# Attention in steps of two groups, with the second mix and the scores on four 64x64 quarters of TensorE

## The chip, the cores and the metric

The kernel runs on one core of one Trainium2 chip. The metric is the device time of one execution in microseconds (us), and the median over several runs is compared. The engines are named as the profile names them: PE (TensorE matmul) and PEld (its weight loads), DVE (VectorE), ACT (ScalarE), POOL (GpSimd) and SP (SyncE, which here only issues DMAs).

## What is computed

An attention with two mixes over the heads, then two feed-forward layers, all in float32 at the interface. There are 4 batches, 12 heads, 448 rows, head dimension 64. The output of the attention is laid out as 1792 rows by 768 columns.

```python
scores = scale * np.matmul(q, k.transpose(0, 1, 3, 2))
scores = np.einsum('bhij,hg->bgij', scores, w_pre)
scores = scores - np.max(scores, axis=-1, keepdims=True)
attn = np.exp(scores)
attn = attn / (np.sum(attn, axis=-1, keepdims=True) + 1e-09)
attn = np.einsum('bhij,hg->bgij', attn, w_post)
x = np.matmul(attn, v)              # then to (1792, 768)
x = (sigmoid(x @ w_gate) * (x @ w_val)) @ w_out
out = np.maximum(x @ w_in2, 0) ** 2 @ w_out2
```

## The kernel before

**Order of the work.** Two programs share the engines. The attention (function attention) is written out by hand as a loop over groups of ten query rows. The two feed-forward layers (function mlp) are built as a list of tasks, and the class Feed emits each task into an engine's queue when its own model of the engines says there is room. During the attention the call feed.step(2.4) after each group (line 448) lets the feed emit 2.4 us worth of its model's time. What it emits there is the preparation of the first layer's weights: loads of raw weights (line 786), two ACT passes (lines 790 and 793), a DVE shift (796), POOL additions (802), DVE or POOL combinations (824) and stores to DRAM (831). The first twelve of these conversions, two halves each, feed the first layer. The layers' own matmuls all stand at line 926 and are not emitted before Feed.finish (line 672) or, on the feed's PE clock, not before that clock is set there.

**Attention, one group at a time.** The 448 rows of a batch are cut into 4 tiles of 100 or 120 rows, ten rows to a group: 45 groups a batch, 180 in all.

- scores (line 188): for one pair of heads and one tile, two float32 matmuls, 64 rows of the array by the tile's 100 or 120 columns, moving 448 columns (line 201). ACT copies one head's result out of PSUM (213), DVE the other's (211), and each goes by one DMA on the SP queue into the buffer g (223), which holds all 12 heads of five query rows on 64 partitions.
- premix (229): the first mix over heads. For two groups at once, four matmuls of 64x64, one in each quarter of the array (237).
- maximum (245), exponent (251), normal (258): row maximum on DVE (248), exp with a sum on ACT (255), sum plus 1e-9 and reciprocal on DVE (260, 263), and the second mixing matrix scaled by the reciprocals on POOL (266).
- postmix (275): the second mix, which also transposes. A group has 128 partitions, two halves of five rows by 12 heads each; the scaled matrix wn is 128 x 120 and is zero where the half of the partitions is not that of the row. Four matmuls with weights of 128 x 112 and 120 moving columns (282). mixed (291) copies the result from PSUM into ap (294).
- values (304): for a chunk of two tiles and a pair of heads, eight matmuls with weights of 112 x 64, moving 240 or 208 columns (311). valued (322) copies on ACT (326) and stores to xs (327).

A float32 matmul shows as two matmul records and two weight loads in the trace. PSUM has eight banks: two for scores (ps_q), four for premix (ps_m), two shared by postmix and values (ps_b).

**What sets the order.** Group s runs premix, maximum(s), exponent(s-1), normal(s-2). Scores and the back part (postmix at least LAG = 3 groups later, and values) are put in by a running budget, left_over, with a cost for each kind of work (lines 29 and 402 to 442). Scores of the next tile are all made LA = 3 groups before the tile begins.

Of the kernel before, what the change touches and what calls it, by code (L numbers as in the profile page):

```python
# [9 lines left out]
F32 = mybir.dt.float32  # L10
# [9 lines left out]
P = 128  # L20
JP = 112
GI = 10
HV = 2
LAG = 3
LA = 3
NA = 9
HB = GI // 2
HP = P // 2
MW, PW, VW, SW, STEP = 0.40, 0.85, 1.66, 0.92, 2.2
# [4 lines left out]
def row_tiles(S):  # L34

    n = -(-S // (2 * GI))
    cuts = [0]
    for t in range(4):
        cuts.append(min(cuts[-1] + (n // 4 + ((0, 1, 3, 2)[t] < n % 4)) * 2 * GI, S))
    return list(zip(cuts, cuts[1:]))  # L40


def columns(i0, i1):

    return 2 * -(-(i1 - i0) // (2 * GI))


def blocks(b, i0, i1):

    n = columns(i0, i1)  # L50
    return [(0, 4), (4, n)] if b == i0 == 0 else [(0, n)]


def row_order(b, i0, i1):

    rows = []
    for g0, g1 in blocks(b, i0, i1):  # L60
        for y in range(2):
            for r in range(HB):
                for g in range(g0, g1):
                    rows.append(min(i0 + (g // 2 * 2 + y) * GI + g % 2 * HB + r, i1 - 1))
    return rows


def attention(tc, feed, q, k, v, w_pre, w_post, xs, B, H, S, D):
# [11 lines left out]
    JT = S // JP  # L80
    NP = H // 2
    SCALE = 1.0 / float(D) ** 0.5

    tiles, groups, chunks = [], [], []
    for b in range(B):
        for t, (i0, i1) in enumerate(row_tiles(S)):
            if t % 2 == 0:
                chunks.append([b, i0, i1, len(groups), 0])
            for g0 in range(i0, i1, GI):
                groups.append((len(tiles), g0 - i0, min(GI, i1 - g0), len(chunks) - 1, g0))  # L90
            chunks[-1][2] = i1
            chunks[-1][4] = len(groups)
            tiles.append((b, i0, i1 - i0))
    NG = len(groups)
    full = [columns(0, t[2]) * GI for t in tiles]
    IM = max(full)
    GT = IM // GI
    CM = max(c[2] - c[1] for c in chunks)
# [3 lines left out]
    with ExitStack() as ctx, ExitStack() as mid, ExitStack() as left:  # L102
        kw = dict(side="right")
        one = ctx.enter_context(tc.tile_pool(name="a_one", bufs=1, **kw))
        pv4 = ctx.enter_context(tc.tile_pool(name="a_v", bufs=4, **kw))
        po = ctx.enter_context(tc.tile_pool(name="a_o", bufs=4, **kw))
        pp = ctx.enter_context(tc.tile_pool(name="a_p", bufs=1, **kw))
        pa = mid.enter_context(tc.tile_pool(name="a_a", bufs=NA, **kw))
        pg = mid.enter_context(tc.tile_pool(name="a_g", bufs=1, **kw))
        ps_b = ctx.enter_context(tc.tile_pool(name="ps_b", bufs=2, space=PSUM, **kw))  # L110
        ps_q = mid.enter_context(tc.tile_pool(name="ps_q", bufs=2, space=PSUM, side="left"))
        ps_m = mid.enter_context(tc.tile_pool(name="ps_m", bufs=4, space=PSUM, side="left"))
        pk = left.enter_context(tc.tile_pool(name="a_k", bufs=KB, side="left"))
        p2 = left.enter_context(tc.tile_pool(name="a_2", bufs=2, side="left"))
        p4 = left.enter_context(tc.tile_pool(name="a_4", bufs=3, side="left"))
# [4 lines left out]
        wq = one.tile([P, H, GI], F32, name="wq")  # L120

        wr = p0.tile([P, 2, H], F32, name="wr")
        mask = p0.tile([P, GI, H], F32, name="mask")
        first = p0.tile([HP, HB, H], F32, name="first")
        g_of = [pg.tile([P, GT, S], F32, name=f"g{m}") for m in range(2)]

        def masks():
# [5 lines left out]
            nc.sync.dma_start(  # L133
                out=wr[G0 : G0 + GI * H, 0, :], in_=w_pre.unsqueeze(0).to_broadcast([GI, H, H])
            )
            for u in range(2):
                nc.sync.dma_start(
                    out=wr[u * HP : u * HP + KH, 1, :],
                    in_=w_post.unsqueeze(0).to_broadcast([HB, H, H]),
                )  # L140
            for u, m in ((0, first), (0, mask[:HP, :HB]), (1, mask[HP:, HB:])):
# [13 lines left out]
        def mixers():  # L155
            for u, m in enumerate((first, mask[HP:, HB:])):
# [9 lines left out]
                in1=wr[:, 1:2, :].to_broadcast([P, GI, H]),  # L166
# [4 lines left out]
        k_t, q_t = {}, {}  # L171
# [5 lines left out]
        def q_load(n, p0=0, p1=NP):  # L177
            if p0 == 0:
                q_t[n] = p2.tile([P, NP, IM], F32, tag="q", name="q")
            n0, isz = sum(full[:n]) * H * D, full[n]  # L180
# [3 lines left out]


        g_t, second = {}, []

        def scores(n, p):

            b, i0, rows = tiles[n]  # L190
            isz = full[n]
            if p == 0:
                g_t[n] = g_of[n % 2]
            kt = k_t.pop((b, p)) if i0 + rows == S else k_t[b, p]
            ps = [
                ps_q.tile([P, S], F32, tag="q", name="ps_s")
                for _ in range(2)
            ]
            for o in range(2):
                r = slice(o * D, (o + 1) * D)  # L200
                nc.tensor.matmul(  # L201
                    ps[o][:isz], lhsT=q_t[n][r, p, :isz], rhs=kt[r], start=True, stop=True
                )
            if n == 0 and p >= 3:
                e = [pa.tile([IM, S], F32, tag="a", name="e0") for _ in range(2)]
            else:
                t = p4.tile([IM, 2, S], F32, tag="e", name="e")
                e = [t[:, o] for o in range(2)]
            for o in range(2):
                if o:  # L210
                    nc.vector.tensor_copy(e[o][:isz], ps[o][:isz])  # L211
                else:
                    nc.scalar.copy(e[o][:isz], ps[o][:isz])  # L213
                e0 = 0
                to = g_t[n][G0 : G0 + GI * H].rearrange("(r h) g j -> h r g j", h=H)
                for m, (g0, g1) in enumerate(blocks(b, i0, i0 + rows)):
                    e1 = e0 + (g1 - g0) * GI
                    move = (to[2 * p + o, :, g0:g1], e[o][e0:e1])
                    if m:
                        second.append(move)  # L220
                    else:
                        queue = nc.scalar if n == 0 and o and p in (1, 3, 4, 5) else nc.sync
                        queue.dma_start(out=move[0], in_=move[1])
                    e0 = e1
# [4 lines left out]
        def premix(s):  # L229
            n, r0 = groups[s][:2]  # L230
            t = r0 // (2 * GI)
            for y in range(2):
                if s + y < NG and groups[s + y][0] == n:
                    a_t[s + y] = ps = ps_m.tile([P, S], F32, tag="m", name="ps_m")
                    r = slice(y * HP, HP + y * KH)
                    for u in range(2):
                        nc.tensor.matmul(  # L237
                            ps[u * HP : (u + 1) * HP],
                            lhsT=wp[r],
                            rhs=g_t[n][r, 2 * t + u],  # L240
                            start=True,
                            stop=True,
                        )

        def maximum(s):
            ps = a_t[s]
            nm = pa.tile([P, 1], F32, tag="nm", name="nm")
            nc.vector.tensor_reduce(out=nm, in_=ps, op=ALU.max, axis=AX.X, negate=True)  # L248
            a_t[s] = [ps, nm]

        def exponent(s):
            ps, nm = a_t[s]
            a = pa.tile([P, S], F32, tag="a", name="a")
            sm = pa.tile([P, 1], F32, tag="sm", name="sm")
            nc.scalar.activation(a, ps, AF.Exp, bias=nm, accum_out=sm)  # L255
            a_t[s] = [a, sm]

        def normal(s):
            sm = a_t[s][1]
            nc.vector.tensor_scalar(  # L260
                out=sm, in0=sm, scalar1=1e-9, scalar2=None, op0=ALU.add
            )
            nc.vector.reciprocal(out=sm, in_=sm)  # L263
            wn = pa.tile([P, H, GI], F32, tag="wn", name="wn")
            if s < NG - 14:
                nc.gpsimd.tensor_scalar(  # L266
                    out=wn, in0=wq, scalar1=sm, scalar2=None, op0=ALU.mult
                )
            else:
                nc.scalar.mul(wn, wq, sm)  # L270
            a_t[s] = [a_t[s][0], wn]

        ap, pending = {}, []

        def postmix(s):
            rows, c = groups[s][2:4]
            if s == chunks[c][3]:
                ap[c] = pp.tile([JP, JT, H, CM], F32, tag="ap", name="ap")
            a, wn = a_t.pop(s)
            ps = ps_b.tile([P, JT, H, GI], F32, tag="b", name="ps_p")  # L280
            for jt in range(JT):
                nc.tensor.matmul(  # L282
                    ps[:JP, jt],
                    lhsT=a[:, jt * JP : (jt + 1) * JP],
# [19 lines left out]
        def values(c, h):  # L304
# [13 lines left out]
            if (h + 2) % HV == 0:  # L318
                del vraw[c, h // HV]
# [945 lines left out]
```

## Time and profile before

| | |
|---|---|
| time before, median of 3 runs | 1388.54 us (1384.6 to 1390.13) |
| the profiled execution | 1390.98 us |
| its span, first to last instruction | 1389.2 us |
| first matmul of the layers in a full stream | about 488 us after the start |
| from there to the end | 901 us |

The span is the part of the execution between the first and the last instruction; 1.8 us of the profiled execution lie outside. In the profile a group of instructions has one row with its count, its busy time and the mean duration of one. Durations of neighbouring matmuls overlap, since the engine is pipelined: where a price is wanted, the distance between starts or the length of a run of matmuls is used, not the mean.

### The profile page before, as it was taken

What the parts mean: (1) busy time and instruction counts of PE and PEld (TensorE: products, weight loads), DVE (VectorE), ACT (ScalarE), POOL (GpSimd) and SP (SyncE); (2) the same over time, 40 slices, a digit from 0 to 9 for tenths busy, and PEclk for the clock granted to TensorE, in tenths of its full rate; (3) what the DMA queues carried; (4) which work ended last, traced back from release to release, by engine and by line L of the source; (5) the groups of instructions that cost most, each with busy time, mean ns of one, the idle gap of its engine ahead of it and who ended that gap; (6) DMA issues with size and microseconds to landing.
All of it is one profiled execution on the core that took longest, in us unless ns stands there. A gap on an engine that the chain in (4) does not pass through costs nothing.

```text
span 1389.2 us, 22066 instructions
## 1 busy us (share of the span) xinstructions
PE 1330.3 (96%) x7602; PEld 1067.5 (77%) x7602; DVE 962.3 (69%) x1828; ACT 709.9 (51%) x1373; POOL 330.1 (24%) x373
## 2 busy tenths in 40 slices
PE   6889999998999899999999999999999999999998
PEld 2445555564655679888999999999888999999998
DVE  2768686695877965677655688848688556898612
ACT  2544455454555655657556563845556445436620
POOL 3233353353444303242323200122231000000000
PEclk9999999999999999999999999999999999999999
DMA  4768878768777567777777742265885344342122
GB/s 153 228 217 249 238 211 269 229 205 256 215 246 222 198 189 271 261 247 260 264 239 253 278 128 57 85 214 171 302 258 195 115 120 142 99 155 58 57 85 80
DMA packets 134362, 268.06 MB, mean 193 GB/s; under 512 B 16684, under 2 KB 79084, under 8 KB 134252
## 3 DMA queue, kind: packets, MB, share of 16 engines
q1 hardware_dynamic: 133872, 266.09, 60.0%
q8 instruction: 60, 0.98, 0.3%
q10 hardware_dynamic: 380, 0.57, 0.1%
q14 instruction: 50, 0.41, 0.1%
HBM read 162.36 MB, written 64.68 MB: 163 GB/s over the span
## 4 chain that ended last, share of the span: by engine, by line
PE 82%; DMA 7%; DVE 7%; ACT 1%; issue 1%; POOL 1%; SPq 0%; DVEq 0%; ACTq 0%; POOLq 0%
PE ps L926 60%; PE ps_p L282 9%; PE ps_s L201 5%; PE ps_m L237 4%; PE ps_v L311 4%; DMA vraw<-in_v 3%; DMA g<-e 3%; DVE ap L294 1%; DVE c L942 1%; DVE w L900 1%; DVE nm L248 1%; DMA gv<-y 1%; DVE c L913 1%; DVE e L211 1%; POOL wn L266 0%
## 5 line engine op out<-in xcount | busy, mean ns | idle before, releaser
L926 PE MATMUL ps<-c,w 128*128 128x448 f32 x4290 | 883.7, 367 | 13.9 <-DVE w L900 6.1
L926 PEld LDWEIGHTS ps<-c,w 128*128 128x128 f32 x4290 | 805.3, 188 | 92.3 <-DVE w L900 10.5
L900 DVE TENSOR_TENSOR w<-w,w 128x768 fp32r<-128x768 f32 x189 | 194.7, 1033 | 173.2 <-ACT w L897 171.8
L802 POOL TENSOR_TENSOR y<-y,raw 128x384 int32<-128x384 int32 x136 | 151.5, 1133 | 433.4 <-DVE y L796 235.6
L897 ACT CAST w<-w 128x768 fp32r<-128x768 f32 x189 | 157.0, 834 | 151.5 <-PE ps L926 138.3
L282 PEld LDWEIGHTS ps_p<-wn,a 128*112 128x112 f32 x1440 | 158.2, 178 | 92.0 <-issue 37.3
L282 PE MATMUL ps_p<-wn,a 128*112 128x120 f32 x1440 | 183.4, 276 | 14.9 <-POOL wn L266 6.7
L913 DVE TENSOR_TENSOR c<-c 128x448 fp32r<-128x448 f32 x280 | 169.1, 647 | 16.2 <-ACT c L910 14.1
L910 ACT CAST c<-c 128x448 fp32r<-128x448 f32 x280 | 143.9, 564 | 55.0 <-DVE c L942 50.8
L266 POOL TENSOR_SCALAR wn<-wq,sm 128x120 f32<-128x120 f32 x166 | 106.5, 642 | 271.0 <-DVE sm L263 207.2
L942 DVE TENSOR_TENSOR c<-ps,c 128x448 f32<-128x448 f32 x172 | 106.6, 622 | 84.4 <-PE ps L926 66.2
L248 DVE TENSOR_REDUCE nm<-ps_m 128x1 f32<-128x448 f32 x180 | 111.0, 617 | 62.0 <-PE ps_m L237 61.7
L255 ACT ACTIVATE a<-ps_m,nm 128x448 f32<-128x448 f32 x180 | 114.5, 636 | 54.2 <-DVE sm L260 43.7
L294 DVE COPY ap<-ps_p 112x480 f32<-112x480 f32 x180 | 114.4, 649 | 18.9 <-PE ps_p L282 17.3
L201 PE MATMUL ps_s<-k,q 64*120 64x448 f32 (+1 forms) x384 | 105.9, 623 | 10.8 <-ACT e L213 5.3
L942 DVE TENSOR_TENSOR c<-c 128x448 f32<-128x448 f32 x184 | 113.0, 647 | 2.4 <-PE ps L926 0.6
L213 ACT COPY e<-ps_s 120x448 f32<-120x448 f32 (+1 forms) x96 | 51.1, 533 | 123.0 <-PE ps_s L201 88.0
L950 ACT COPY c<-ps 128x448 f32<-128x448 f32 x128 | 67.7, 534 | 76.7 <-PE ps L926 74.0
L237 PE MATMUL ps_m<-g,wp 64*64 64x448 f32 x720 | 94.2, 584 | 5.1 <-DMA g<-e 3.8
L311 PE MATMUL ps_v<-ap,vraw 112*64 112x240 f32 (+1 forms) x768 | 84.2, 365 | 10.5 <-DMA vraw<-in_v 9.7
L311 PEld LDWEIGHTS ps_v<-ap,vraw 112*64 112x64 f32 x768 | 54.5, 139 | 51.2 <-issue 15.0
L211 DVE COPY e<-ps_s 120x448 f32<-120x448 f32 (+1 forms) x96 | 60.0, 625 | 47.3 <-PE ps_s L201 29.6
(34 smaller groups left out, 535.3 us busy)
## 6 DMA issues: line engine op xcount, KB each, us to landing
w<-gv SPq DMA_DIRECT2D x84, 384.0 KB
g<-e SPq DMA_DIRECT2D x132, 210.0 KB
raw<-in_wo SPq DMA_DIRECT2D x56, 384.0 KB
w<-wi SPq DMA_DIRECT2D x56, 384.0 KB
w<-wo SPq DMA_DIRECT2D x49, 384.0 KB
wo<-y SPq DMA_DIRECT2D x42, 384.0 KB
gv<-y SPq DMA_DIRECT2D x36, 384.0 KB
raw<-in_wi SPq DMA_DIRECT2D x32, 384.0 KB
```

The costliest lines, as they stand in the source:

```text
L201: nc.tensor.matmul(ps[o][:isz], lhsT=q_t[n][r, p, :isz], rhs=kt[r], start=True, stop=True)
L237: nc.tensor.matmul(ps[u * HP : (u + 1) * HP], lhsT=wp[r], rhs=g_t[n][r, 2 * t + u], start=True, stop=True,)
L282: nc.tensor.matmul(ps[:JP, jt], lhsT=a[:, jt * JP : (jt + 1) * JP], rhs=wn.rearrange("p g i -> p (g i)"), start=True, stop=True,)
L294: nc.vector.tensor_copy(ap[c][:, :, :, g0 - i0 : g0 - i0 + rows], ps[:JP, :, :, :rows])
L311: nc.tensor.matmul(ps[o * D : (o + 1) * D, :w], lhsT=vraw[c, (h + o) // HV][:, (h + o) % HV, jt, :], rhs=ap[c][:, jt, h + o, :w], start=jt ...
L802: e.tensor_tensor(out=y3, in0=y3, in1=of(raw.tile.bitcast(I32)[:, :, 0])[:, i], op=ALU.add)
L897: e.copy(dst.tile[:, 0], flat())
L900: e.tensor_tensor(out=dst.tile[:, 1], in0=flat(), in1=dst.tile[:, 0].bitcast(F32), op=ALU.subtract)
L910: e.copy(hi.tile, src.tile)
L913: e.tensor_tensor(out=lo.tile, in0=src.tile, in1=hi.tile.bitcast(F32), op=ALU.subtract)
L926: e.matmul(bank.tile, lhsT=a[k], rhs=x[l], start=start and n == 0, stop=stop and n == 2, skip_group_check=more,)
L942: e.tensor_tensor(out=out.tile, in0=a.tile, in1=b.tile, op=op)
```

## The change

The attention is rewritten; the layers stay as they are.

- **Tiles and steps.** The work goes in steps of two groups (20 rows), 23 a batch and 92 in all. Batch 0 has five tiles of 3, 5, 5, 5 and 5 steps, the others four of 6, 6, 6 and 5: 17 tiles.
- **Scores** run as four matmuls of 64 rows by at most 64 columns, one in each quarter. After the first tile and part of the second, one ACT copy takes both heads out of PSUM (896 elements a partition); DVE no longer copies any. The DMAs into g stay as they were, two to a pair of heads.
- **Maximum, sum and reciprocal** are one DVE instruction for both groups of a step; exp stays at two a step.
- **Second mix.** The scaled matrix is 128 x 60 without its zero blocks. A step has 28 matmuls with weights of 64 x 64 and 60 moving columns: 7 blocks of 64 keys, 2 halves, 2 groups. One DVE copy of 960 elements a partition replaces two of 480. The result has 128 keys to a partition block instead of 112, with the keys of the last block filled up.
- **Values** take one tile and six heads at a time: 24 matmuls, weights 128 x 64, moving 120 columns (100 for a tile of five steps), and one ACT copy of three pairs. There are two such units a tile, 34 in all. The loads of v are two a batch instead of twelve.
- **PSUM.** Premix has two pairs of banks. Postmix, values and scores take turns on two other pairs (next_turn), in the order in which they are written.
- **Order.** The budget is gone. A fixed plan gives a step its scores (by the length of the tile before: 2, 2, 1, 1, 0, 0 or 2, 2, 1, 1, 0 or 1, 1, 0) and its values (in the fourth and fifth step of the next tile). Within a step TensorE gets premix, postmix of three steps before, values, scores.
- **Feed.** It gets 3.8 us of its model's time a step, from the fourth step on, and 1.5 us in each of twelve steps behind the last. The layers' matmuls may be emitted from the last step on. Four of the layers' PSUM banks come free at that point, where six did; the number of cells handed over early is 20 where it was 23.

```diff
+STEP = 2 * GI
+LAG = 3
+NA = 4
+EB = 4
...
+    lengths = [n // 4 + (t < n % 4) for t in range(4)]
+    if b == 0:
+        lengths = [3] + [(n - 3) // 4 + (t < (n - 3) % 4) for t in range(4)]
...
+        ps_t = ctx.enter_context(tc.tile_pool(name="ps_t", bufs=1, space=PSUM, **kw))
+        ps_m = mix.enter_context(tc.tile_pool(name="ps_m", bufs=2, space=PSUM, side="left"))
...
+        turns = [ps_t.tile([P, 2, BANK], F32, name=f"turn{m}") for m in range(2)]
...
+        def scores(n, p, ps, early=False):
...
+            for c in range(0, isz, HP):
+                c1 = min(c + HP, isz)
+                for o in range(2):
+                    r = slice(o * D, (o + 1) * D)
+                    nc.tensor.matmul(
+                        ps[c:c1, o, :S], lhsT=q_t[n][r, p, c:c1], rhs=kt[r], start=True, stop=True
+                    )
...
+                nc.scalar.copy(e[:isz], ps[:isz, :, :S])
...
+        def postmix(s):
+            n, t, ys = steps[s]
+            a, wn = a_t.pop(s)
+            ps = next_turn()
+            out = ps[:, :, : JT * 2 * KH].rearrange("p u (j y x) -> p u j y x", j=JT, y=2)
+            for y in ys:
+                for j in range(JB):
+                    c = j % 2 * HP
                     for u in range(2):
+                        r = slice(u * HP, (u + 1) * HP)
                         nc.tensor.matmul(
+                            out[c : c + HP, u, j // 2, y],
+                            lhsT=a[r, y, j * HP : (j + 1) * HP],
+                            rhs=wn[r, y].rearrange("p g i -> p (g i)"),
                             start=True,
                             stop=True,
                         )
...
+            for m in range(VP):
+                for j in range(JT):
+                    for o in range(2):
+                        nc.tensor.matmul(
+                            ps[o * D : (o + 1) * D, 0, m * 2 * c : (m + 1) * 2 * c],
+                            lhsT=vt[:, 2 * m + o, j],
+                            rhs=x[:, j, :, (i * VP + m) * 2 + o],
...
+            spread = {3: (1, 1, 0), 5: (2, 2, 1, 1, 0), 6: (2, 2, 1, 1, 0, 0)}[s1 - s0]
...
+            if 3 <= s < NS:
+                feed.step(3.8)
+            elif s >= NS:
+                feed.step(1.5)
...
-        self.free["PE"] = self.now
+        self.free["PE"] = max(self.free["PE"], self.now)
```

## Rows read from the trace of the kernel before

**Rows 1.** The page: the span, and each engine's busy time and share.

```profile
span 1389.2 us, 22066 instructions
PE 1330.3 (96%) x7602; PEld 1067.5 (77%) x7602; DVE 962.3 (69%) x1828; ACT 709.9 (51%) x1373; POOL 330.1 (24%) x373
```

**Rows 2.** Windows: length; PE, PEld, DVE, ACT, POOL busy; clock; DMA share; GB/s.

```profile
45.00:440.00 395.00, 372.31 (x2806) 219.94 (x2804) 294.88 (x767) 198.26 (x485) 158.17 (x216) 0.98 0.75 231
...
488.00:1389.00 901.00, 883.62 (x4290) 805.20 (x4290) 611.23 (x932) 470.79 (x789) 138.11 (x116) 1.00 0.54 176
```

**Rows 3.** The chain that ended last, by line, from the page.

```profile
PE ps L926 60%; PE ps_p L282 9%; PE ps_s L201 5%; PE ps_m L237 4%; PE ps_v L311 4%; DMA vraw<-in_v 3%; DMA g<-e 3%; DVE ap L294 1%; DVE c L942 1%; DVE w L900 1%; DVE nm L248 1%; DMA gv<-y 1%; DVE c L913 1%; DVE e L211 1%; POOL wn L266 0%
```

**Rows 4.** Groups by form, 45 to 440 us: busy, mean ns, idle before and releaser.

```profile
L282 PE MATMUL ps_p<-wn,a 128*112 128x120 f32 x1232 | 157.2, 276 | 8.7 <-POOL wn L266 4.9 <-DVE ap L294 3.3
L282 PEld LDWEIGHTS ps_p<-wn,a 128*112 128x112 f32 x1232 | 135.5, 178 | 76.1 <-issue 35.0 <-POOL wn L266 29.6 <-POOL y L802 8.1
...
L255 ACT ACTIVATE a<-ps_m,nm 128x448 f32<-128x448 f32 x156 | 99.3, 637 | 52.8 <-DVE sm L260 43.0 <-PE ps_p L282 6.3 <-DVE sm L263 1.5
L248 DVE TENSOR_REDUCE nm<-ps_m 128x1 f32<-128x448 f32 x157 | 96.9, 617 | 52.9 <-PE ps_m L237 52.7
L294 DVE COPY ap<-ps_p 112x480 f32<-112x480 f32 x151 | 96.2, 651 | 15.7 <-PE ps_p L282 14.3
...
L211 DVE COPY e<-ps_s 120x448 f32<-120x448 f32 x60 | 37.5, 625 | 21.7 <-PE ps_s L201 11.8 <-DMA g<-e 6.8 <-DMA k<-in_k 1.1
L213 ACT COPY e<-ps_s 120x448 f32<-120x448 f32 x60 | 32.0, 533 | 65.9 <-PE ps_s L201 45.4 <-DMA g<-e 12.0 <-issue 6.8
L255 ACT ACTIVATION_READ_ACCUMULATOR a<-ps_m,nm 128x1 f32 x156 | 31.1, 200 | 0.0
...
L263 DVE RECIPROCAL sm<-sm 128x1 f32<-128x1 f32 x157 | 25.7, 164 | 5.4
...
L790 ACT ACTIVATE raw<-raw 128x768 f32<-128x768 f32 x24 | 22.0, 917 | 0.0
...
L237 PEld LDWEIGHTS ps_m<-g,wp 64*64 64x64 f32 x316 | 15.7, 134 | 16.7 <-issue 8.8 <-ACT a L255 1.4
...
L326 ACT COPY xo<-ps_v 128x240 f32<-128x240 f32 x20 | 7.2, 360 | 26.2 <-PE ps_v L311 19.9 <-issue 5.6 <-ACT a L255 0.7
```

**Rows 5.** Pieces of the chain in order of time: start, length (us), what.

```profile
19.44 2.68 DMA g<-e
...
55.14 7.79 DMA g<-e
...
319.42 1.77 PE ps_v L311 x16
...
342.42 1.82 PE ps_p L282 x16
...
347.16 1.00 PE ps_p L282 x8
```

**Rows 6.** Timeline of PE, 338 to 352 us: start, length, records of one kind.

```profile
345.24 0.98 PE L237 MATMUL ps_m<-g,wp 64*64 64x448 f32 x8
346.15 1.02 PE L201 MATMUL ps_s<-k,q 64*120 64x448 f32 x4
347.09 1.07 PE L282 MATMUL ps_p<-wn,a 128*112 128x120 f32 x8
```

**Rows 7.** Timeline cut to what starts from 345.230 to 345.262 us.

```profile
345.23 0.15 PEld L237 LDWEIGHTS ps_m<-g,wp 64*64 64x64 f32 x4
345.24 0.61 PE L237 MATMUL ps_m<-g,wp 64*64 64x448 f32 x4
```

**Rows 8.** Timeline of the first premix, 22.5 to 24.4 us.

```profile
22.58 1.77 PE L237 MATMUL ps_m<-g,wp 64*64 64x448 f32 x8 [3.83 <-DMA g<-e]
```

**Rows 9.** Instructions of the scores' copies: duration ns min/median/max, first and last start.

```profile
L223 SPq DMA_DIRECT2D g<-e x188: 748/762/1698, 7.8 to 442.6; - x188
```

More of the change, by code (lines that the diff above doesn't have):

```diff
@@ L79, in attention @@
     nc = tc.nc
-    JT = S // JP
     NP = H // 2
+    JB = S // HP
+    JT = -(-JB // 2)
     SCALE = 1.0 / float(D) ** 0.5
-    tiles, groups, chunks = [], [], []
+    VP = 3
+    tiles, steps, starts = [], [], []
     for b in range(B):
[L86 to L93, printed above, removed]
@@ L94, in attention @@
-    NG = len(groups)
-    full = [columns(0, t[2]) * GI for t in tiles]
-    IM = max(full)
+        for i0, i1, length in row_tiles(b, S):
+            lead = skipped(i0, i1, length)
+            starts.append(len(steps))
+            for t in range(length):
+                steps.append((len(tiles), t, [y for y in range(2) if y * length * GI + (t + 1) * GI > lead]))
+            tiles.append((b, i0, i1, length, lead))
+    NT, NS = len(tiles), len(steps)
+    starts.append(NS)
+    sizes = [t[3] * STEP for t in tiles]
@@ L183, in q_load @@
             nc.sync.dma_start(out=q_t[n][:, p0:p1, :isz], in_=x[:, p0:p1])
[L186 to L198, printed above, removed]
-            for o in range(2):
[L200 to L224, printed above, removed]
@@ L273, in attention @@
[L273 to L284, printed above, removed]
-                    rhs=wn.rearrange("p g i -> p (g i)"),
-                    start=True,
-                    stop=True,
-                )
-            pending.append((mixed, s, ps))
@@ L322, in valued @@
-        def valued(c, h, ps):
-            b, i0, i1 = chunks[c][:3]
-            w = i1 - i0
-            xo = po.tile([P, CM], F32, tag="xo", name="xo")
-            nc.scalar.copy(xo[:, :w], ps[:, :w])
-            nc.sync.dma_start(out=xs[b][h * D : (h + 2) * D, i0:i1], in_=xo[:, :w])
-            if i1 == S and h + 2 == H:
-                feed.fire(("x", b))
-        NT = len(tiles)
-        starts = [next(s for s in range(NG) if groups[s][0] == n) for n in range(NT)] + [NG]
-        k_order = iter([(b, p) for b in range(B) for p in range(NP)])
@@ L384, in attention @@
-        for s in range(NG + 30):
-            if s < NG and groups[s][1] // GI % 2 == 0:
+            scores(0, p, [*spare, *turns][p % 4], True)
+            if p == 0:
+                mixers()
+        for p in range(NP - sum(x[0] == "scores" for s in range(starts[1]) for x in plan[s])):
+            scores(1, p, next_turn())
+        q_load(2)
+        k_next = {}
+        for n in range(NT):
+            if not last_of(n) or n + 1 == NT:
+                continue
+            b = tiles[n][0] + 1
+            first_free = KB - NP
+            for p in range(NP):
+                at = starts[n - 1] + 1 + p // 2 if p < first_free else starts[n - 1] + 2 + p // 2
+                k_next.setdefault(at, []).append((b, p))
@@ L439, in attention @@
[L439 to L449 removed]
+            if 1 <= s <= NS:
+                exponent(s - 1)
+                if s == NS:
+                    mix.close()
+                    low.close()
+                    feed.widen(1)
+                    feed.free["PE"] = feed.now
@@ new lines, in attention @@
+            after = []
+            if LAG <= s < NS + LAG:
+                after.append(postmix(s - LAG))
+            for x in k_next.get(s, ()):
+                k_load(*x)
+            for x in v_next.get(s, ()):
+                v_load(*x)
+            units = plan[s]
+            for f, *x in units:
+                if f == "values":
+                    after.append(values(*x))
+                    while len(after) > 1:
+                        after.pop(0)()
+            for f, *x in units:
+                if f == "scores":
+                    if after:
+                        after.pop(0)()
+                    n, p = x
+                    scores(n, p, next_turn())
+                    if p == NP - 1 and n + 2 < NT:
+                        q_load(n + 2)
+                    if n == NT - 1 and p == NP - 1:
+                        left.close()
+                        closed = True
+                        feed.widen(0)
```

360 lines of the change are left out of this document (162 added, 198 removed).

## The prediction

> **What bounds the kernel now.** The page comes first: of a span of 1389.2 us PE is busy 96%, and no other engine over 69% [rows 1]. That is a mean over two stages, so the windows come next [rows 2]. From 488 us on only the two layers run: 901 us with PE busy 883.6. The change leaves them as they are, so what it can win lies ahead of 488 us. In the attention's body, 45 to 440 us, PE is busy 372 of 395 us, DVE 295, ACT 198, POOL 158, the DMA engines 75%, at a granted clock of 0.98. The chain that ended last says the same [rows 3]: after the layers' matmuls, the second mix is the longest line (9%), then the scores, the first mix and the values; DMA takes some 7%. In the groups by form [rows 4] nearly every group on ACT and DVE waits for PE, and PE's second mix waits only 8.7 us in all. So the attention is bound by TensorE, with DVE some way behind.
>
> **The price of a column.** The 16 records of two second mixes in a row take 1.82 us and the 8 records of one take 1.00 [rows 5], so 8 more records of 120 columns cost 0.82 us: 0.103 us each, 0.85 ns a column. Sixteen records of the values, two column halves side by side, give the same: 8 x 240 x 0.85 ns is 1.64 us of their 1.77. A score or a first mix, two records of 448 columns in each part of the array, is then 0.77 us. From start to start they take 0.91 and 0.94 us [rows 6], so each change of shape costs some 0.15 us. The price of a weight load follows from 178 ns for 112 columns and 134 ns for 64 [rows 4]: 0.92 ns a column, 0.059 us for 64.
>
> **The second mix, which carries the sum.** Removed: 16 records a step, 1.82 us. Added: 28 matmuls, so 56 records, of 60 columns (0.051 us) with loads of 64 (0.059 us), over four quarters. The fullest quarter has 16 records. If the quarters work side by side and each hides a load behind the matmul before it, it takes 16 x 0.059 = 0.94 us; by columns alone it would be 0.82. If they do not work side by side, it is 56 x 0.059 = 3.3 us. The nearest row is the first mix, of the same 64 x 64 shape: its eight records, four quarters by two, take 0.98 us [rows 6], while one after another they would need 8 x 448 x 0.85 ns = 3.1 us. So I take 0.94, and keep 0.82 and 3.3 as ends.
>
> **A rule against it.** Can so many short matmuls be issued? The first mix's four matmuls all start between 345.230 and 345.262 us, with their four loads [rows 7]: at most 11 ns apart. At that distance the 56 records need 0.6 us and issue is no bound. The Trainium skill, TensorE: Matmul & The Clock Gate, section "Wait — 56ns, not 53.3ns?", says that start-to-start "never drops below ≈25 ns however small N is"; by that the step's second mix would be at least 1.4 us. The trace speaks against it for different quarters, but shows no run of more than four starts. I go by the row.
>
> **The other work on PE, for a step.** First mix 0.77; a score 0.77, and with the second mix now of the same shape the 0.15 us between them goes. A unit of values is 24 matmuls in two column halves, 24 records a half of 120 columns: 2.46 us, and 0.3 for the two changes of shape, 2.76. The columns are as before; only records and loads double, and 0.059 hides behind 0.103.
>
> **ACT.** Two exps with their sum reads, 2 x (0.637 + 0.200) = 1.67 us a step [rows 4]. A score's one copy of 896 elements lies between 0.53 (as the copy of 448) and 1.07 (two of them); 0.533 for 448 and 0.360 for 240 elements give 0.83 ns an element, so 0.91. The values' copy of 360 elements is 0.46 by the same slope. The weight conversions' 24 halves, two passes of 0.917 us, are 44 us, or 0.48 a step.
>
> **DVE and POOL.** DVE loses the scores' copies (0.625 us each, off PE's path already). What stays is at most 2 x 0.617 for the maximum, 2 x 0.651 for the copy out of the second mix and about 0.3 for the sums, 2.85 us a step; joined instructions save some of that and the conversions add some: I take 3.0. POOL was idle more than half of the time [rows 2] and its matrices shrink by half; nothing is charged.
>
> **The steps of a tile.** PE and ACT are not loaded in the same steps, and PE can be only some two steps ahead of ACT (two pairs of banks for the first mix), so a step costs about what its busiest engine does:
> - first and second step, two scores each: PE 0.77 + 0.94 + 1.54 = 3.25, ACT 1.67 + 1.82 + 0.48 = 3.97. ACT, 3.97.
> - third, one score: PE 2.48, ACT 3.06.
> - fourth, a score and values: PE 0.77 + 0.94 + 0.77 + 2.76 = 5.24.
> - fifth, values: PE 4.47.
> - sixth, neither: PE 1.71, DVE 3.0.
>
> A tile of six steps is 23.7 us, of five 20.7, the first one of three some 9.3. Nine, seven and one of them give 213 + 145 + 9 = 367 us.
>
> **What is late next.** A tile's first mix needs all 12 heads in g. After a tile of five steps the last score is written at the end of its fourth step; then come the copy (0.91), two issues on SP at 0.762 us each [rows 9] and a transfer that takes 2.7 to 7.8 us in the chain [rows 5]: 5.1 to 10.2 us, of which only the fifth step, 4.47, is cover. After a tile of six, 7.5 us cover it. That is 0.6 to 5.7 us on seven tiles and 0 to 2.7 on nine, 4 to 64 us in all. The DMA engines have a quarter of their time left [rows 2], and the same bytes move in less of it; most landings should be nearer the short end, so I take 18. On SP, a score's DMA still stands behind loads of k, q, v and raw weights; these are issued without long waits, and v's are now few.
>
> **Both ends.** The first premix starts at 22.6 us [rows 8], after 3.8 us of waiting for DMA. Four scores of the second tile now stand ahead of it: between nothing, if they fill that wait, and 4 x 1.77, the early pace of this row; 26 us. Behind the last step there are three second mixes and two units of values, 8.3 us, partly beside the layers' first matmuls, which may now start there: 5 us. The conversions get less of the feed's time (89 x 3.8 = 338 us of its model against 172 x 2.4 = 413), so perhaps two of twelve are left for the layers. The layers use one conversion in each quad, so the last are wanted late; charged at nothing, and at 10 us if that cover is gone. The layers' start with four banks instead of six: nothing, up to 3 us.
>
> **The sum.** 26 + 367 + 18 + 5 = 416 us where the layers began at 488: 72 us less. Against the profiled execution's own 1390.98 us that is 1319; this execution lies 2.4 us above the median, so **1317**.
>
> **Rivals.**
> 1. *PE alone decides.* If steps even out, so that ACT's heavy steps hide under PE's, the tiles cost PE's sums: 20.4, 18.7 and 6.7, 321 us, and with 26 and 5 the attention is 352 us: 1253. For it: PE is the busiest by far now. Against: two pairs of banks for the first mix are little slack. 0.12.
> 2. *Issue.* Starts 25 ns apart make the second mix 1.4 us. That adds 0.46 us only in the two steps a tile that PE sets, 32 of them: 15 us, 1332. It is the rule cited above. 0.05.
> 3. *The two turns.* Second mix, scores and values share two bank pairs; the third user in a step waits until the first is copied out, and these copies stand behind exps on ACT and behind the maximum on DVE. If no copy were covered, the steps would be 6.4, 6.4, 4.7, 7.9, 6.2 and 3.0, 34.6 instead of 23.7: 1.8 us a step, 167 us. With a third of that on the path the time is 1373: 0.16. For it: before, scores had banks of their own and still ACT's copies of them waited 12.0 us for a DMA to free their buffer [rows 4].
> 4. *Slower, by the same turns.* The gain of 72 us is eaten when over 43% of those copies lie on the path; at half, 1400: 0.09. It decides in the steps with two scores, where ACT does the exps and both copies in order.
> 5. *The quarters do not work side by side,* so that the change does not do what it says: 3.3 us for the second mix, 1.8 us a step by the same table, 167 us more: 1484. Against it stand rows 6. 0.06.
>
> **How the numbers follow.** The forecast has 0.52: between 1290 and 1345 by its own unknown terms. What the runs can tell from no change is about 0.5%, 7 us. Faster: the forecast, rivals 1 and 2 and most of 3, 0.81; within: 0.05; slower: rivals 4 and 5, 0.14. The range 1268 to 1395 leaves out most of rival 1 below, and rival 5 and half of 4 above.
>
> **What would show it.** Right: the layers' full stream starts near 416 us and lasts 901 as before; the second mix's 56 records of a step lie within about 1 us; ACT is busy over 80% in the attention and PE under 90%; short waits of the first mix for g at a tile's start. Wrong: second mixes of 1.4 us or more, PE waiting for ACT's or DVE's copies in each step (rivals 3 and 4), or PE back at 95% (rival 1). If the layers took much over 901 us, the charge of nothing for the conversions would be the error.

## The result and the profile after

The changed kernel takes 1402.93 us (median of 3 runs, 1398.87 to 1403.79) against 1388.54: the ratio is 1.0102, with a 95% interval of 1.0057 to 1.0147. It is slower by 1%, where 1317 was forecast and 1268 to 1395 given. The profiled run took 1398.87 us.

The page of the changed kernel first: span, busy time, PE's share in 40 slices and the granted clock.

```profile
span 1397.1 us, 31155 instructions
...
PE 1249.2 (89%) x12474; PEld 1043.0 (75%) x12474; DVE 879.2 (63%) x1399; ACT 736.6 (53%) x1351; POOL 288.9 (21%) x380
...
PE   4786787778688799999999999999999999999998
...
PEclk8898898999899999999999999999999999999999
```

Against [rows 1], PE has 81 us less to do and the span is 8 us longer: the work did go, and idle time took its place. The windows say where; the columns are those of [rows 2].

```profile
45.00:440.00 395.00, 303.79 (x7113) 198.50 (x7104) 216.44 (x374) 220.10 (x475) 109.68 (x203) 0.90 0.68 209
...
488.00:1397.00 909.00, 884.85 (x4266) 804.55 (x4266) 619.41 (x951) 477.00 (x796) 150.80 (x129) 0.99 0.56 181
```

In the attention's body PE is busy 77% of the time (before 94%), and of the others only ACT has more to do than before (220 us against 198). PE is not the bound any more, and nothing else is. In the page's groups (busy, mean ns, idle of the engine before them and what ended it) one line stands out, the first mix:

```profile
L226 PE MATMUL ps_m<-g,wp 64*64 64x448 f32 (+1 forms) x720 | 96.7, 594 | 84.8 <-DMA gv<-y 26.2
...
L211 ACT COPY e<-turn 120x896 f32<-120x896 f32 (+1 forms) x96 | 86.8, 908 | 136.6 <-issue 63.5
L277 PEld LDWEIGHTS turn<-wn,a 64*64 64x64 f32 x5040 | 113.7, 145 | 53.8 <-issue 49.7
...
L277 PE MATMUL turn<-wn,a 64*64 64x60 f32 x5040 | 113.5, 233 | 7.5 <-issue 7.5
...
L295 DVE COPY ap<-turn 128x960 f32<-128x960 f32 x88 | 101.4, 1152 | 19.7 <-PE turn L277 19.2
```

PE stood idle 84.8 us before first mixes; before the change all idle time ahead of the same line was 5.1 us:

```profile
L237 PE MATMUL ps_m<-g,wp 64*64 64x448 f32 x720 | 94.2, 584 | 5.1 <-DMA g<-e 3.8 <-DMA gv<-y 1.3
```

It comes at the start of a tile, when the first mix needs all twelve heads in g. From the trace, in us, for the first step of each tile after the first: from the end of the last score's copy to the issue of its second DMA, from that issue to the first mix, and PE's idle time.

```
tile (steps)     1(5) 2(5) 3(5) 4(5) 5(6) 6(6) 7(6) 8(5) 9(6) 10(6) 11(6) 12(5) 13(6) 14(6) 15(6) 16(5)
copy to issue     2.2  0.9  0.9  2.9  6.4  0.9  1.0  3.3  0.9   2.4   3.5   0.9   2.4   0.9   0.9   0.9
issue to mix      5.9  6.7  4.5  6.5  9.0  6.0  7.7  7.9  9.4   6.4   7.6   5.2  11.6   6.6   4.8   5.6
PE idle           7.8  1.1  2.6  6.2 12.6  2.1  3.6  4.8  7.0   4.1   6.0   1.0  10.8   2.8   0.5   1.2
```

With 0.9 at the very first tile the idle times come to 75 us. Which transfer a row names as the one that ended a wait is inferred, and several transfers share a semaphore: a row of the first mix may name gv or q. The semaphores' own updates settle it. At each of the 16 tiles the last update of the semaphore of the tile's last transfer into g comes 0.13 to 0.56 us ahead of the first mix, so it is g that is waited for. From issue to that update (its landing) the transfer took 4.4 to 11.2 us, median 6.1.

The longest wait, at the first tile of the second batch, is worth following. PE's timeline of it (start, length, records):

```profile
129.98 1.10 PE L277 MATMUL turn<-wn,a 64*64 64x60 f32 x56
131.00 2.28 PE L312 MATMUL turn<-ap,v 128*64 128x100 f32 x48
145.84 1.77 PE L226 MATMUL ps_m<-g,wp 64*64 64x448 f32 x8 [12.56 <-DMA gv<-y]
```

What SP issued meanwhile:

```profile
128.43 1.59 SPq L215 DMA_DIRECT2D g<-e  x2
130.13 0.42 SPq L806 DMA_DIRECT2D gv<-y  x1
130.66 1.18 SPq L761 DMA_DIRECT2D raw<-in_wg  x2
131.89 0.67 SPq L192 DMA_DIRECT2D v<-in_v  x1
132.86 0.44 SPq L328 DMA_DIRECT2D xs<-xo  x1
135.48 2.14 SPq L215 DMA_DIRECT2D g<-e  x2
```

And the two copies on ACT around the last score:

```profile
128.54 0.41 ACT L326 COPY xo<-turn 128x300 f32<-128x300 f32 x1 [1.36 <-PE turn L312]
129.51 0.91 ACT L211 COPY e<-turn 120x896 f32<-120x896 f32 x1 [0.57 <-PE turn L203]
```

The last score is copied out by 130.4, but its DMAs come out at 135.5: a store of converted weights, two raw loads, a load of v and a store of the values stand ahead. That is not all: from 133.3 to 135.4 SP issued nothing. It waited for the load of v that it had issued eight transfers earlier, at 127.28, and whose semaphore the next transfer into g uses again; it landed at 135.42. SP's waits from 129 to 140 us show it:

```profile
SPq L215 <- DMA v<-in_v: 2.1, 1, 2.1
```

The last transfer into g landed at 145.28, and the first mix ran at 145.84. In that stretch the DMA engines were 90% busy and PE's granted clock 0.71:

```profile
130.00:147.00 17.00, 4.44 (x116) 3.63 (x112) 2.87 (x5) 3.31 (x10) 0.88 (x3) 0.71 0.90 285
```

So the waits have three sources that only runs can part: too little lead in the plan, the conversions on the same SP queue, and the bytes in flight.

### The profile page after: what moved, and what is told of

It reads as the page before. It is cut to its first block, busy times and chain, and to the rows that moved or that the text cites. A ratio compares the mean times of both kernels' runs of the same rounds, so it can differ in the third digit from the quotient of the medians.

```text
span 1397.1 us, 31155 instructions
## 1 busy us (share of the span) xinstructions
PE 1249.2 (89%) x12474; PEld 1043.0 (75%) x12474; DVE 879.2 (63%) x1399; ACT 736.6 (53%) x1351; POOL 288.9 (21%) x380
## 4 chain that ended last, share of the span: by engine, by line
PE 58%; DVE 3%; ACT 1%; issue 1%; DMA 1%; DVEq 0%; SPq 0%; ACTq 0%
PE ps L901 58%; DVE w L875 2%; DVE c L917 1%; ACT w L872 1%; DVE c L888 0%; DMA wo<-y 0%; DMA w<-wi 0%; ACT raw L765 0%; DMA spill<-c 0%; ACT c L885 0%; DVE c L1052 0%; ACT c L925 0%; ACT ps L925 0%; ACT c L927 0%; DVE y L771 0%
## 5 line engine op out<-in xcount | busy, mean ns | idle before, releaser
L901 PE MATMUL ps<-c,w 128*128 128x448 f32 x4290 | 890.9, 369 | 24.4 <-DVE w L875 11.2
L242 DVE TENSOR_REDUCE nm<-ps_m 128x2 f32<-128x896 f32 (+1 forms) x92 | 98.4, 1070 | 173.8 <-PE ps_m L226 173.4
L226 PE MATMUL ps_m<-g,wp 64*64 64x448 f32 (+1 forms) x720 | 96.7, 594 | 84.8 <-DMA gv<-y 26.2
L211 ACT COPY e<-turn 120x896 f32<-120x896 f32 (+1 forms) x96 | 86.8, 908 | 136.6 <-issue 63.5
L277 PEld LDWEIGHTS turn<-wn,a 64*64 64x64 f32 x5040 | 113.7, 145 | 53.8 <-issue 49.7
L262 POOL TENSOR_SCALAR wn<-wq,sm 128x60 f32<-128x60 f32 x180 | 75.2, 432 | 334.7 <-DVE sm L259 232.9
L203 PE MATMUL turn<-k,q 64*64 64x448 f32 (+3 forms) x776 | 106.1, 603 | 18.0 <-DVE ap L295 12.2
L277 PE MATMUL turn<-wn,a 64*64 64x60 f32 x5040 | 113.5, 233 | 7.5 <-issue 7.5
L295 DVE COPY ap<-turn 128x960 f32<-128x960 f32 x88 | 101.4, 1152 | 19.7 <-PE turn L277 19.2
L312 PE MATMUL turn<-ap,v 128*64 128x120 f32 (+2 forms) x1632 | 84.6, 261 | 1.3 <-DVE ap L295 1.3
L312 PEld LDWEIGHTS turn<-ap,v 128*64 128x64 f32 x1632 | 77.4, 139 | 4.0 <-DVE ap L295 1.4
```

Of the source, the lines that this page charges most:

```text
L203: nc.tensor.matmul(ps[c:c1, o, :S], lhsT=q_t[n][r, p, c:c1], rhs=kt[r], start=True, stop=True)
L226: nc.tensor.matmul(ps[u * HP : (u + 1) * HP, y, :S], lhsT=wp[r], rhs=g_of[n % 2][r, 2 * t + u], start=True, stop=True,)
L277: nc.tensor.matmul(out[c : c + HP, u, j // 2, y], lhsT=a[r, y, j * HP : (j + 1) * HP], rhs=wn[r, y].rearrange("p g i -> p (g i)"), start=True,
L312: nc.tensor.matmul(ps[o * D : (o + 1) * D, 0, m * 2 * c : (m + 1) * 2 * c], lhsT=vt[:, 2 * m + o, j], rhs=x[:, j, :, (i * VP + m) * 2 + o] ...
L901: e.matmul(bank.tile, lhsT=a[k], rhs=x[l], start=start and n == 0, stop=stop and n == 2, skip_group_check=more,)
```

## The experiments

The idle time is that at the starts of the tiles; the attention's end is that of its last matmul; "layers" runs from their 51st matmul record to the start of the last one. These three times are us of the one profiled run of each kernel; the whole times of one kernel's runs differ among themselves by 5 to 21 us, so a few us in one of these columns say little. Ratios are against the kernel before, each on its own chip.

```
kernel                         idle  att. end  layers   ratio (95%)
before                          5.1    488.0    886.2
changed                        74.9    485.2    894.4   1.0102 (1.0057 to 1.0147)
e1 scores a step earlier       39.6    449.9    897.5   0.9828 (0.9780 to 0.9877)
e2 no conversions              57.2    440.9    938.0   one run, 1430.48 us
e3 last scores on ACT's queue  57.3    475.2    893.1   0.9965 (0.9930 to 1.0001)
e4 e1, feed 4.6                57.9    476.7    887.1   0.9870 (0.9812 to 0.9928)
e5 e1, v later                 35.2    443.2    900.4   0.9807 (0.9753 to 0.9861)
e6 two steps earlier            4.9    428.9    901.8   0.9704 (0.9665 to 0.9743)
e7 e6, v later                  8.5    439.4    895.8   0.9722 (0.9682 to 0.9761)
e8 e7, feed 4.6                 7.4    454.8    912.4   0.9817 (0.9747 to 0.9887)
e9 e6, feed 4.2                 7.5    449.8    898.7   0.9784 (0.9744 to 0.9823)
e10 e6, feed 3.4               10.9    444.8    896.4   0.9780 (0.9749 to 0.9810)
```

**e1: the last scores a step earlier.**

```diff
-            spread = {3: (1, 1, 0), 5: (2, 2, 1, 1, 0), 6: (2, 2, 1, 1, 0, 0)}[s1 - s0]
+            spread = {3: (2, 0, 0), 5: (2, 2, 2, 0, 0), 6: (2, 2, 2, 0, 0, 0)}[s1 - s0]
```

> The changed kernel's scores of the next tile come 2, 2, 2, 0, 0, 0 (or 2, 2, 2, 0, 0) instead of 2, 2, 1, 1, 0, 0: the last one a step earlier, by some 4 us. Theory (the first mix at a tile's start waits for the last scores' transfers into g, because these stand behind other transfers; 75 us of such waits on PE in the changed kernel, 0.5 to 12.6 us a tile): a wait shrinks by up to the step gained, so 75 us become 25 to 35, the last matmul of the attention moves from 485 us to about 445, and the time falls by 30 to 45 us, less what the layers give back. Rival (ACT and the two turns set the pace, the waits only fill time that ACT or DVE would need anyway): a third step with two scores on ACT makes steps longer by what the waits lose, and the time stays within 10 us.

Measured: 1373.56 us, ratio 0.9828. The idle time fell from 75 to 40 us, a little less than expected, and the attention ended 35 us sooner. PE's first mix, in the groups of this run:

```profile
L226 PE MATMUL ps_m<-g,wp 64*64 64x448 f32 (+1 forms) x720 | 92.1, 572 | 44.7 <-DMA v<-in_v 14.7 <-DMA gv<-y 7.9 <-ACT a L250 6.4
```

The waits were on the path one for one: 35 us less idle, 35 us sooner. The rival, that they hide time which ACT needs anyway, falls.

**e2: no conversions during the attention.** The layers' weights are then prepared behind it.

```diff
-            if 3 <= s < NS:
-                feed.step(3.8)
-            elif s >= NS:
+            if s >= NS:
                 feed.step(1.5)
```

> The changed kernel with no weight conversions during the attention: all twelve come behind its last step. The plan of the scores is as in the changed kernel. Theory (the last scores' transfers are late because the conversions' loads and stores stand ahead of them on the SP queue and in the transfers): from the last issue into g to the first mix it is about 3 us instead of 4.5 to 11.6, the waits at the tiles' starts fall from 75 to under 20 us and the attention ends near 415 us. Rival (the plan leaves too little time even on an empty queue): waits of 50 us or more stay. Rival (the copies on ACT are late): the time from the last copy to the first mix is unchanged. In all cases the layers start starved, and the whole takes longer than the changed kernel by some 50 to 150 us; that says nothing of the theories.

Measured: one run of 1430.48 us, the layers starved as expected. The theory's number was missed: 57 us of waits stayed, not under 20, and the attention ended at 441, not 415.

```profile
L226 PE MATMUL ps_m<-g,wp 64*64 64x448 f32 (+1 forms) x720 | 93.6, 576 | 59.7 <-issue 19.1 <-DMA v<-in_v 10.7 <-DMA q<-in_q 10.0
```

From copy to issue it is now 0.9 us at every tile but one, so the conversions do hold up the SP queue; but from issue to first mix it still takes 3.9 to 8.6 us within a batch and 10.3 to 11.9 at a batch's first tile, where the two loads of v are issued shortly ahead of the last score's transfers. The conversions made 18 of the 75 us of waits. Most of the waiting is the plan's: it gives too little lead even without them. (The attention ended 44 us sooner; besides the 18, some 21 us came out of the steps themselves and 6 from the end.) So the theory of a crowded queue fell as the main cause, and the rival took its place.

**e3: the last two scores of a tile on ACT's DMA queue.**

```diff
-                queue = nc.scalar if early and o and p < NP - 1 else nc.sync
+                queue = nc.scalar if (early and o and p < NP - 1) or (not early and p >= NP - 2) else nc.sync
```

> The changed kernel with the transfers of a tile's last two scores issued from ACT's queue instead of SP's; the bytes, the plan and the conversions are unchanged. Theory in its narrow form (the transfers stand behind others in one queue in order): they no longer stand behind anything, the time from copy to first mix falls to 3 to 5 us, and the waits fall from 75 to 15 to 30 us, against 4 issues of 0.78 us more on ACT a tile; the time falls by 25 to 45 us. Theory in its wide form (the DMA engines are shared by all queues, the transfers wait for the bytes in flight whatever their queue): waits of 45 us or more stay, and with ACT's issues the time moves by less than 15 us.

Measured: ratio 0.9965, so some 19 us less than the changed kernel's 1.0102, between the two expectations. 57 us of idle stayed. ACT issues the pair right behind the copy, at all but three tiles within 1.0 us; its timeline at one of them:

```profile
298.90 0.91 ACT L211 COPY e<-turn 120x896 f32<-120x896 f32 x1 [0.47 <-PE turn L203]
299.84 1.65 ACTq L215 DMA_DIRECT2D g<-e  x2
```

Yet from issue to first mix it is still 3.4 to 10.0 us, median 6.7, as in the changed kernel (6.5), and to the landing 3.1 to 9.8, median 6.2 (6.1). A queue of its own saves the place in line on SP (18 us, as much as taking the conversions away) and not the transfer: the wide form holds. The Trainium skill (DMA: Bandwidth & Descriptors, "Queues, rings and completion order") says that SP's and ACT's queues feed the same 16 DMA engines, and that a transfer's signal lands only after every earlier write of its DMA engine, across queues. The medians agree; which of the two it is, the run does not show.

**e4: e1 with more time for the feed.**

```diff
-                feed.step(3.8)
+                feed.step(4.6)
```

> As e1, and the feed gets 4.6 us of its model's time a step instead of 3.8, so that the conversions of the changed kernel that were left for the layers (two of twelve, stored at 517 and 533 us) are done in the attention. Theory: the layers lost 8 to 11 us to those two conversions; here they take as long as in the kernel before, and the gain of e1 is kept: 5 to 15 us faster than e1. Rival: more transfers in the attention make the waits for g longer by as much, and it is not faster than e1.

Measured: ratio 0.9870, not faster than e1. Both sides were right about their part. All twelve conversions were stored by 461 us, and the layers took 887 us as before the change, 10 less than in e1. But the waits rose from 40 to 58 and the attention ended 27 us later.

**e5: e1 with the loads of v behind the first steps of the new batch.**

```diff
-                v_next[starts[n] + 2] = [(tiles[n + 1][0], 0)]
-                v_next[starts[n] + 3] = [(tiles[n + 1][0], 1)]
+                v_next[starts[n + 1] + 2] = [(tiles[n + 1][0], 0)]
+                v_next[starts[n + 1] + 4] = [(tiles[n + 1][0], 1)]
```

> As e1, and the two loads of v of a new batch (768 KB each) are issued in the third and fifth step of the new batch's first tile instead of the third and fourth of the tile before, so not between the scores and the first mix of a batch's first tile. Theory (a tile's first transfers into g share the DMA engines with what was issued around them): the waits at the three starts of a batch, 7.8, 3.3 and 6.2 us in e1, fall to 0 to 3 us, the sum of the waits from 40 to 25 to 32 us, and the time by 5 to 13 us against e1. Rival (the lead alone decides): the three waits stay.

Measured: 0.9807 against 0.9828 for e1, within each other's intervals. The waits at the three starts went from 7.8, 3.3 and 6.2 to 5.5, 1.0 and 2.5 us, in the direction expected, but others grew; the sum fell by 4 only.

**e6: the scores two steps earlier.** The plan begins in the last step of the tile before the one before; the first tiles are as in e1.

```diff
-            s0, s1 = starts[n - 1], starts[n]
-            spread = {3: (1, 1, 0), 5: (2, 2, 1, 1, 0), 6: (2, 2, 1, 1, 0, 0)}[s1 - s0]
+            s0, s1 = starts[n - 1] - (n > 1), starts[n]
+            spread = (2, 2, 2) if n > 1 else (2, 0, 0)
...
-        for p in range(NP - sum(x[0] == "scores" for s in range(starts[1]) for x in plan[s])):
+        for p in range(NP - sum(x[:2] == ("scores", 1) for s in range(starts[1]) for x in plan[s])):
```

> As e1, with the scores of the third and later tiles a whole step earlier again: two in the last step of the tile before the one before, two in the first and two in the second step of the tile before; the first tiles as in e1. Theory now (without any conversions the time from the last score's copy to the first mix was still 5.1 to 12.8 us, so the plan of the changed kernel gives too little lead even on an empty queue; it is the lead that costs most): the waits fall from 40 us in e1 to 10 to 20, most of it at the second tile, whose scores are not moved; the attention ends 15 to 25 us sooner than in e1 and the time is 10 to 25 us under e1. Rival (waits are made up elsewhere: the steps from the first mix on are bound by ACT): the waits go and the attention ends within 5 us of e1.

Measured: 1354.22 us, ratio 0.9704, the fastest of all. The waits are gone, to 5 us, and the attention ends at 429. A window of the attention's body, here to 400 us (in the same window the changed kernel's PE is busy 270 us at a clock of 0.89), and the first mix:

```profile
45.00:400.00 355.00, 302.96 (x7416) 200.73 (x7412) 224.82 (x387) 228.29 (x495) 113.79 (x210) 0.98 0.77 243
```

```profile
L226 PE MATMUL ps_m<-g,wp 64*64 64x448 f32 (+1 forms) x720 | 91.7, 570 | 30.3 <-ACT a L250 26.1 <-DMA gv<-y 1.7 <-DMA q<-in_q 1.1
```

The clock is at 0.98 as before the change, and what idle time is left ahead of the first mix waits for an exp on ACT, not for a DMA. The last transfer into g takes no less from issue to landing than in the changed kernel (5.4 to 9.3 us, median 6.5), but from tile 5 of the table above on it lands 2.4 to 9.1 us ahead of the first mix. With the same second mix, the same conversions and the same bytes, the lead alone turns a loss of 1% into a gain of 3%. Not all of the 70 us came back: the steps without waits took 382 us, 16 more than in the changed kernel (366), and why was not tried.

**e7 and e8: e6 with v later, and that with 4.6 us of feed.** The edits are those of e5 and e4.

> e5 and e6 together. Theory: waits under 12 us, and the time 0 to 8 us under e6, since with the earlier scores most of the waits at the starts of a batch are gone already.

> As e7, with 4.6 us of the feed's model time a step instead of 3.8, so that all twelve conversions are done in the attention. Theory: with lead enough, the additional transfers cost no waits at the tiles' starts any more, the layers take 887 us from their 50th matmul to the end as in the kernel before instead of 897, and the time is 0 to 10 us under e7. Rival: the conversions' ACT and DVE work makes the steps longer by as much or more (e2 showed 345 us for the steps without conversions and 365 with ten of them), and it is not faster than e7.

Measured: e7 has 0.9722, no different from e6. e8 has 0.9817, slower by its median, though the intervals touch: its runs lie between 1363 and 1385 us, and the profiled one, 1384, is among the longest. In that one the waits stayed at 7 us as the theory said, but the attention took 15 us more than in e7, and the layers did not come back to 887 us but took 912. The second is not explained: all twelve conversions were stored by 457 us, and of the 17 us over e7's layers 13 come between the 2000th and 3000th matmul record (226 us against 213).

**e9 and e10: the feed's time around 3.8.** e6 with 4.2 and with 3.4 in the same line as e4.

> As e6, with 4.2 us of the feed's model time a step instead of 3.8. In e6 the layers take 902 us from their 50th matmul to the end, 16 more than in the kernel before, because some of the twelve conversions are left for them. If that is the only thing in play, one more conversion in the attention gives 3 to 8 us back. If the steps are bound by ACT and DVE, whose conversion work it adds to (20 us for ten conversions by e2 and the changed kernel, so 2 us for one), some of that goes again: between 6 us faster and 4 us slower than e6.

> As e6, with 3.4 us instead of 3.8: one conversion fewer in the attention. By the same two prices the attention ends 2 to 6 us sooner and the layers take 5 to 10 us longer: 0 to 8 us slower than e6. If it were faster than e6, the conversions would cost the attention more than they save the layers.

Measured: 0.9784 and 0.9780, both 0.8% over e6, some 11 us by the ratios. Both are outside what was expected, and so is e10's attention, which ended 16 us later than e6's with one conversion fewer. The feed's pace is not a smooth dial: more and less of it were both slower. It moves every conversion's place between the attention's own instructions; that this is what cost the time was not tried.

## Why the prediction was wrong, step by step

**What bounds it, and the second mix: right.** In the trace of the changed kernel the 56 records of a step lie within 0.88 or 0.89 us from first to last start in 48 of the 88 full steps, where 0.94 was forecast. Two steps with two scores each, from the timeline of PE:

```profile
118.29 0.93 PE L226 MATMUL ps_m<-g,wp 64*64 64x448 f32 x8
119.04 1.04 PE L277 MATMUL turn<-wn,a 64*64 64x60 f32 x54
119.87 0.59 PE L203 MATMUL turn<-k,q 64*56 64x448 f32 x2
...
121.50 0.98 PE L203 MATMUL turn<-k,q 64*64 64x448 f32 x8 [0.60 <-DVE sm L258]
122.30 0.93 PE L226 MATMUL ps_m<-g,wp 64*64 64x448 f32 x8
```

From first mix to first mix it is 4.01 us, forecast 3.97; no 0.15 us is lost between first mix, second mix and scores. Rivals 2 and 5 fall: the 56 records start 16 ns apart on average. That is less than the 25 ns of the Trainium skill (TensorE: Matmul & The Clock Gate, "Wait — 56ns, not 53.3ns?"), so where quarters alternate the rule does not hold here. The copy of 896 elements took 0.908 us (0.91 forecast), the copy of 960 on DVE 1.15.

**The steps: the sum right, the reason not.** First to last first mix is 465.2 - 24.8 = 440.4 us; less the 74 us of waits behind the first tile, 366. Forecast: 367 with the last step's 4.5, so 362.5. Part of that is luck. The prediction said that a step with two scores costs what ACT needs, 3.97 us. The second step of tiles 1 to 15 took 4.01 or 4.02 us in 13 of 15 cases, but ACT was busy only 3.1 us of it in the median. In all 15 PE waited 0.60 to 0.93 us ahead of the second score, which started 0.05 to 0.06 us after DVE's copy out of the second mix; DVE's timeline of the first of the two steps above (118.2 to 122.4 us) has the copy's end at 121.45, and the score starts at 121.50:

```profile
119.29 1.09 DVE L242 TENSOR_REDUCE nm<-ps_m 128x2 f32<-128x896 f32 x1 [1.58 <-PE ps_m L226]
120.30 1.15 DVE L295 COPY ap<-turn 128x960 f32<-128x960 f32 x1
```

So the pair of banks that the second mix and this score share set the length of these steps, with the copy behind the maximum on DVE: the mechanism of rival 3, in one place. The third steps agree: eight of fifteen took 2.45 to 2.50 us, PE's sum of 2.48 and not ACT's 3.06. And where over 80% was named for ACT as a sign of being right, it was busy 56% of the body (220 of 395 us), and 64% in e6 without the waits. Other errors cancel: the first step of tiles 1 to 15 took 5.2 us on average where 3.97 were forecast, and a sixth step 2.05 where 3.0 were.

**What is late next: here it failed.** This step of the prediction gave 4 to 64 us and took 18, "most landings should be nearer the short end". It was 75, above the upper end. Three parts were mis-sized.

- The transfer. The 18 us stand for a transfer of about 4.6 us behind its issue (7 x 2.6 us, and nothing after six steps), so 5.4 from the issue's start. It took 4.4 to 11.2 from there, median 6.1, and to the first mix 4.5 to 11.6, median 6.5. The 2.68 us of [rows 5] is from the start, with the DMA engines 40% busy (17 to 23 us) against 68% in the changed body.
- The queue. "These are issued without long waits" was false for SP: from the copy's end to the second issue it took up to 6.4 us, 1.9 on average, where the first issue alone is 0.76.
- The cover. After a tile of six steps PE had 6.1 us of other work from the end of the last score (median), not 7.5. One of the seven tiles counted with 4.47 us follows the tile of three steps and had 2.9; it waited 7.8.

The trace of before held the answer and I did not look: there the later of the last score's two copies ended 8.3 to 15.0 us ahead of the tile's first mix, median 10.4. The last transfer took much the same as now, 3.5 to 7.9 us, median 5.9, but landed 0.5 to 8.5 us early, and PE hardly waited. The plan of the change left its first mix to run a median of 8.4 us after that copy, waits included. e6 shows the cause: with more lead 70 us of the waits and 56 us of the attention go.

**Both ends: partly.** The first premix came at 24.8 (26). From the last first mix to the attention's end it was 20.0 us where 9.5 were forecast (the last step's 4.5 and 5): second mixes and values of the end, with the layers' first matmuls in between.

**The conversions, charged at nothing: mis-sized.** Ten of twelve were stored before the attention's end, the last at 517 and 533 us. From 485.2 to the end it was 912 us, 11 over the 901 forecast. e4 fits this: with all twelve done the layers took 887 us, against 897 in e1 and 894 here. But e8 took 912 with all twelve done, and e10 896 with fewer done than e6, which took 902. So what is left of the conversions is not the whole of it, and this part stays open.

**The sum.** Over the forecast of 416 us the attention has -1 at the start, +56 for waits behind the first tile, +4 in the steps, +10 at the end: 485. With +11 for the layers that is 80 us over 416 + 901 = 1317, the 1397 us of the span. Rivals 3 and 4 named a mechanism that is there, but not at their size: PE lost 18.0 us ahead of scores, 12.2 of it for DVE's copy, and the steps kept the forecast length. That rival 4 named nearly the time (1400) is luck. Rival 1 fell as well: the two-score steps took 4.01 us and not PE's 3.25.

## What to carry to other kernels

When an engine gets faster, the transfers that it hid need not get shorter (here a median of 5.9 us before, 6.1 after, 6.5 in e6): measure the lead that the old kernel gives each transfer, from the last producer to the first user, and keep it in microseconds, not in steps. A fixed plan that shortens the step shortens every lead with it; here two steps more were worth 4% with the same work. A step time that comes out as forecast does not show that the engine named as its limit is the limit: look at what the waiting engine starts behind. Of the work that other engines do in the shadow of a stage (here weight conversions) less fits when the stage gets shorter; what the rest costs behind it was not settled here.

## What was not expected of the hardware

A wait cost more than its length. In the 17 us around the wait of 12.6 us the granted clock was 0.71 on average, so part of it at the lower of the two levels, 1.2 GHz; PE had been idle most of that time. Right behind it the first mix took 1.77 us (above) and the second mix 1.83, where in the steady steps they took 0.93 and 1.04. The timeline's row of that second mix:

```profile
147.36 1.83 PE L277 MATMUL turn<-wn,a 64*64 64x60 f32 x54
```

Over the whole body the mean clock was 0.90 with the waits and 0.98 without them (e6).
